# Local values in three key blocks of 96 rows by one load each, and the first expert loads a step later: a sparse attention with a mixture of experts on one core

## Chip, cores and metric

The kernel runs on one core of one Trainium2 chip. The metric is the device time of one execution in microseconds; before the change its median over three runs was 573.74 us (573.61 to 576.4).

## What is computed

Attention over 8 batches, 8 heads, 576 positions and head dimension 64, all in float32; then each token (4608 of 512 columns) goes to one of 8 experts, a two-layer network with a ReLU.

```python
mask_local = (rel >= 0) & (rel < 32)                      # heads 0 to 3
mask_strided = (rel >= 0) & (pos[None, :] % 32 == pos[:, None] % 32)   # heads 4 to 7
attn = softmax(where(mask, q @ k.T / 8, -1e9));  x = attn @ v
logits = x @ w_gate + modality_bias[modality_id];  e = argmax(logits)
out = softmax(logits)[e] * (relu(x @ w1[e]) @ w2[e])
```

A query of a local head sees 32 keys: those up to itself in its own block of 32, and the rest in the block before. A query of a strided head sees the 18 positions with its own remainder by 32.

## The kernel before

The program has two stages. In the first, attention is done in 32 units: for each of the four pairs of batches (`NBP`), four heads of `Local` and four units of `Strided`, in turns (even units are local, odd ones strided). TensorE's order is written out by hand: the loop `for n in range(nu + 3)` runs 35 steps, and step n holds the scores of unit n, the turning (transposes) of unit n - 2, the masks of unit n + 1 and the values of unit n - 3. Between these lie five places, 0 to 4; at places 0 to 3 `spot(n, place)` calls `fetch`, which issues the loads that the table `FETCH` names for that place, and `slot`. `pop` puts in pieces of `finish_pair` and `route`, which turn a finished pair of batches into token rows, compute the routing of its tokens and scatter them to `xd` in memory. The other engines are ordered by the scheduler, by its own estimate of times; the instructions inside `pin` keep the program's order.

In `FETCH`, "12a" and "12b" are the two halves (64 rows each) of unit 12's q and k, "12v" the first half of its values and "12w" the second half. Each load is issued on SyncE's queue (SP) and is `paced`: it waits for the last TensorE instruction ahead of it in the program. The values of a strided unit are one load of 128 rows; those of a local unit are two, over the odd and over the even rows.

A local unit's values (`vl`) are laid out in 18 windows of 65 columns (64 and a column of ones, which gives the sum of the weights). A window holds the 32 keys of the block before and the 32 of its own block. Windows of two neighbouring blocks lie above each other in 64 + 64 rows: block j - 1, block j, block j, block j + 1, so that block j is there twice. In `turn` of `Local`, the exponentials `ex` are transposed into PSUM (`t1` for 16 blocks, `t2` for the two left over), and ScalarE (ACT) copies them into `et` and `e8`, in which the first window's columns fill rows 0 to 63 and the second's rows 64 to 127; the rest of these tiles was set to zero once. `values` multiplies them by `vv`:

```python
et[r, :, :, par, :] <- t1[r]              # r = 64 rows, par = 0, 1
o[64 * jj:64 * jj + 64, k, :] = et[:, ...].T @ vv[:, 4 * k + 2 * jj + bb, :]
```

`SPOTS` says at which places a `slot` does something: it issues a piece of the scatter, or, once the first routing tables are known (`calm`), the next of ten pieces of `early`: the first experts' weights (`raws[0]` to `raws[3]`; the last two share their tiles with `lqk`) and the first tokens (`fx`). Steps 32 to 34, if not in the table, have places 1, 2 and 4.

The second stage runs the experts in blocks of 256 or 512 tokens (`ffn`), with each float32 operand split in a high and a low part: `h` (L1052) and `o` (L1070) are its matmuls, `wh` and `wl` (L1094, L1097) and, for the first block, `ws` (L975) the split weights.

Of the kernel before, what the change touches and what calls it, by code (L numbers as in the profile page):

```python
# [20 lines left out]
P = 128  # L21
B, H, S, D = 8, 8, 576, 64
STRIDE = 32
NBP = 4
# [15 lines left out]
LT, RK = 3, (13, 6)  # L40
SPOTS = {
    15: (2, 3, 4,), 16: (0, 1,), 18: (1,), 19: (2, 3, 4,), 23: (2, 3,), 25: (1, 2, 3,), 27: (2, 3, 4,), 28: (0,),
    29: (1, 2, 4,), 30: (0, 1,), 31: (1, 2, 4,),
}
FETCH = {
# [9 lines left out]
}  # L55
LAG = 2
FIRST, SECOND, SPLIT, SEND, GATHER, FAR = 1, 3, 4, 6, 7, 6
CPAD = 1216
BIG = -float(2 ** 30)
# [77 lines left out]
def _layout(q, k, v, moe_modality_id, moe_w_gate, moe_modality_bias, moe_w1, moe_w2):  # L137
    q, k, v = (np.asarray(t, np.float32) for t in (q, k, v))

    def local_t(t):
        return t[:, :4].reshape(NBP, 2, 4, S, D).transpose(0, 2, 1, 4, 3).reshape(NBP, 4, 2, D, 18, 32)

    qt, kt = local_t(q), local_t(k)
    vr = v[:, :4].reshape(NBP, 2, 4, 18, 32, D).transpose(0, 2, 1, 3, 4, 5)
    qkl = np.zeros((NBP, 4, 2, D, 37, 32), np.float32)
    win = np.zeros((NBP, 4, 2, 64, 18, D + 1), np.float32)
    win[..., D] = 1
    for bb in range(2):  # L150
        for i in range(18):
            blk = _block(i, bb)
            qkl[:, :, bb, :, i] = qt[:, :, bb, :, blk]
            qkl[:, :, bb, :, 19 + i] = kt[:, :, bb, :, blk]
            w = win[:, :, i % 2, :, 2 * (i // 2) + bb]
            w[:, :, 32:, :D] = vr[:, :, bb, blk]
            if blk:
                qkl[:, :, bb, :, 18 + i] = kt[:, :, bb, :, blk - 1]
                w[:, :, :32, :D] = vr[:, :, bb, blk - 1]
    qkl = np.stack([qkl[:, :, 1], np.concatenate([qkl[:, :, 0, :, 18:], qkl[:, :, 0, :, :18]], axis=-2)], axis=2)  # L160
    qkl = qkl.reshape(NBP, 4, P, 37 * 32)
    vl = win.reshape(NBP, 4, P, 18 * (D + 1))

    def strided_t(t):
        t = t[:, 4:].reshape(B, 2, 2, 18, 32, D).transpose(0, 1, 2, 5, 4, 3)
        return np.ascontiguousarray(t).reshape(B, 2, 2, D, S)

    qs, ks = strided_t(q), strided_t(k)
    qks = np.stack([np.concatenate([qs[:, :, 1], ks[:, :, 1]], axis=-1), np.concatenate([ks[:, :, 0], qs[:, :, 0]], axis=-1)],
                   axis=2).reshape(B, 2, P, 2 * S)  # L170

    vr = v[:, 4:].reshape(B, 2, 2, 18, 32, D)
    vs = np.zeros((B, 2, P, 10, D), np.float32)
    va = vr[:, :, :, :, 0:28].reshape(B, 2, 2, 18, 4, 7, D).transpose(0, 1, 5, 3, 4, 2, 6)
    vs[:, :, 0:126, 0:8] = va.reshape(B, 2, 126, 8, D)
    vb = vr[:, :, :, :, 28:32].transpose(0, 1, 4, 3, 2, 5)
    for u in range(4):
        vs[:, :, 32 * u:32 * u + 18, 8:10] = vb[:, :, u]
    vs = vs.reshape(B, 2, P, 10 * D)

    w1 = np.asarray(moe_w1).reshape(E, 4, P, 8, P).transpose(0, 3, 2, 1, 4).reshape(E, 8, P, 512)
    w2 = np.asarray(moe_w2).reshape(E, 8, P, DM)
    w = np.concatenate([w1, w2], axis=-1).reshape(E, 4, 2, P, 1024).transpose(0, 1, 3, 2, 4).reshape(E * 4 * P, 2048)

    wg = np.zeros((P, 4, 32), np.float32)
    wg[:, :, :E] = np.asarray(moe_w_gate).reshape(4, P, E).transpose(1, 0, 2)
    mod = np.ascontiguousarray(moe_modality_id).astype(np.int64).view(np.int32).reshape(NT, 2)[:, 0]
    mod = mod.reshape(36, P).transpose(1, 0)
    mb = np.broadcast_to(np.asarray(moe_modality_bias).reshape(1, 2 * E), (P, 2 * E))
    cf, cb, cr, tok = _constants()  # L190
    cz = np.concatenate([wg.reshape(P, 4 * 32), mb.astype(np.float32), np.ascontiguousarray(mod).view(np.float32),
                         tok.view(np.float32), np.ascontiguousarray(cr).view(np.float32)], axis=1)
    assert cz.shape == (P, Z_N)
    nul = np.zeros((SLOT, ROW), np.int32)
    nul[:, DM] = NT
    arrays = {
        "qkl": qkl, "vl": vl, "qks": qks, "vs": vs, "w": w,
        "cz": cz, "cf": cf, "cb": cb, "nul": nul.view(np.float32),
    }
    return {n: np.ascontiguousarray(t) for n, t in arrays.items()}  # L200
# [14 lines left out]
def attention_moe(ctx: ExitStack, tc: tile.TileContext, a, out):  # L215
# [140 lines left out]
    class Local:  # L356
# [7 lines left out]
            self.qk = lqk[n % 2]  # L364
            return load_qk(self.qk.rearrange("p x i q -> p (x i q)"), S + 32, a["qkl"][self.bp, self.h], part)

        def load_values(self, part):
            n = self.n
            if not part:
                self.vv = lp.tile([P, 18, D + 1], F32, tag="vv", name=f"vv{n}")  # L370
            return pin(nc.sync.dma_start(
                self.vv.rearrange("p i d -> p (i d)")[part:P:2], a["vl"][self.bp, self.h, part:P:2]))

        def masks(self):
            self.sp = []
# [40 lines left out]
        def turn(self):  # L416
            n, ex = self.n, self.ex
            self.et = et = ets[n % 2]
            t1 = pa(f"t1{n}").rearrange("p (g q) -> p g q", g=4)
            for k in range(4):  # L420
                turned_to(t1[:, k, :], ex[:, 2 * k:2 * k + 2, :])
            t2 = pa(f"t2{n}")[:, 0:P]
            turned_to(t2, ex[:, 8:10, :])
            for par in range(2):
                r = slice(64 * par, 64 * par + 64)
                nc.scalar.copy(et[r, :, :, par, :], t1[r].rearrange("p k (u q) -> p k u q", u=4))
            self.e8 = e8 = e8s[n % 2]
            for jj in range(2):
                r = slice(64 * jj, 64 * jj + 64)
                nc.scalar.copy(e8[r, :, jj, :], t2[r, r].rearrange("p (b q) -> p b q", b=2))  # L430

        def values(self):
            n, et, e8, vv, xt, h = self.n, self.et, self.e8, self.vv, self.xt, self.h
            for bb in range(2):
                gn = 5 - bb
                o = pa(f"o{n}{bb}")[:, :(D + 1) * gn].rearrange("p (g c) -> p g c", g=gn)
                for k in range(4):
                    for jj in range(2):
                        nc.tensor.matmul(  # L439
                            o[64 * jj:64 * jj + 64, k, :],  # L440
                            et[:, 2 * (k // 2) + bb, 2 * (k % 2) + jj, :, :].rearrange("p g q -> p (g q)"),
                            vv[:, 4 * k + 2 * jj + bb, :],
                            start=True, stop=True, skip_group_check=True,
                        )
                if bb == 0:
                    for b2 in range(2):
                        nc.tensor.matmul(
                            o[64 * b2:64 * b2 + 64, 4, :], e8[:, b2, :, :].rearrange("p j q -> p (j q)"),
                            vv[:, 16 + b2, :], start=True, stop=True, skip_group_check=True,
                        )  # L450
                rs = lp.tile([P, 5], F32, tag="rs", name=f"rs{n}{bb}")
                nc.vector.tensor_scalar(rs[:, :gn], o[:, :, D], 1e-9, None, ALU.add)
                nc.vector.reciprocal(rs[:, :gn], rs[:, :gn])
                nc.vector.tensor_tensor(
                    xt[bb][:, :, D * h:D * h + D], o[:, :, 0:D],
                    rs[:, :gn].unsqueeze(2).to_broadcast([P, gn, D]), ALU.mult,
                )

    class Strided:
# [7 lines left out]
            self.qk = sqk[n % 2]  # L467
            return load_qk(self.qk.rearrange("p i q -> p (i q)"), S, a["qks"][self.b, self.pr], part)

        def load_values(self, part):  # L470
            n = self.n
            self.vs = lp.tile([P, 10, D], F32, tag="vs", name=f"vs{n}")
            return pin(nc.sync.dma_start(self.vs.rearrange("p g d -> p (g d)"), a["vs"][self.b, self.pr]))
# [756 lines left out]
    def fetch(n, place):  # L1230

        for item in FETCH.get((n, place), "").split():
            u, part = units[int(item[:-1])], "abvw".index(item[-1])
            paced(u.load(part) if part < 2 else u.load_values(part - 2))

    for i in range(3):
        for part in range(2):
# [116 lines left out]
```

## Time and profile before

| | |
|---|---|
| runs | 573.61, 573.74, 576.4 us |
| the profiled execution | 577.81 us, its span 575.7 us |
| TensorE (PE), matmuls | 546.1 us busy, 95% |
| VectorE (DVE) | 378.6 us, 66% |
| ScalarE (ACT) | 312.2 us, 54% |
| GpSimd (POOL) | 89.0 us, 15% |
| data moved by DMA | 137.00 MB, 238 GB/s |
| mean granted clock of TensorE | 0.987 |

An engine's busy share is a mean over stages with different limits, so stages are looked at one by one. A wait is named by the engine, the line, and what ended it; "issue" is time in which the engine waited for nothing that the profile shows. PEld is TensorE's weight load, which runs beside its matmuls. The names behind a line are the tile written, an arrow, and the tiles read.

### The profile page before, as it was taken

How to read it: one execution, taken by the hardware profiler on the slowest of the kernel's cores; microseconds unless marked ns; L12 is line 12 of the kernel's file. 1: busy time of each engine (PE TensorE's matmuls, PEld its weight loads, DVE VectorE, ACT ScalarE, POOL GpSimd, SP SyncE). 2: the span in 40 equal slices, each digit the busy share in tenths (PEclk: the TensorE clock that was granted, in tenths of full speed). 3: DMA queues.
4: the chain of work that ended last, by engine and by line, in shares of the span. 5: the costliest groups of instructions: out<-in, count | busy, mean ns of one | idle time of the engine just before them, and what ended most of it. 6: DMA issues, size and time to landing. Idle time of an engine off the chain costs nothing.

```text
span 575.7 us, 13499 instructions
## 1 busy us (share of the span) xinstructions
PE 546.1 (95%) x5273; PEld 463.0 (80%) x5273; DVE 378.6 (66%) x940; ACT 312.2 (54%) x651; POOL 89.0 (15%) x108
## 2 busy tenths in 40 slices
PE   6888798898999999999999999999999999999995
PEld 3677687776888999899888888888888888889984
DVE  7886877868977996777875626735734634547541
ACT  3476586676776666666643344343353353356642
POOL 2020212320603511011010020020020020021320
PEclk9899999998999999999999999999999999999998
DMA  8888988989999999998996672582482543455621
GB/s 290 271 287 295 309 279 285 303 313 370 389 322 282 317 367 347 356 304 233 309 248 245 141 266 78 147 275 91 128 253 95 153 178 111 128 202 174 246 92 40
DMA packets 65942, 137.00 MB, mean 238 GB/s; under 512 B 40383, under 2 KB 40767, under 8 KB 58816
## 3 DMA queue, kind: packets, MB, share of 16 engines
q1 hardware_dynamic: 59168, 112.46, 61.1%
q0 software_dynamic: 6416, 23.37, 11.0%
q8 instruction: 43, 0.70, 0.5%
q10 hardware_dynamic: 288, 0.24, 0.1%
q14 instruction: 27, 0.22, 0.1%
HBM read 107.97 MB, written 24.30 MB: 230 GB/s over the span
## 4 chain that ended last, share of the span: by engine, by line
PE 86%; issue 4%; DVE 4%; ACT 3%; DMA 1%; POOL 0%; SPq 0%; POOLq 0%; DVEq 0%; ACTq 0%
PE h L1052 35%; PE o L1070 35%; PE o L439 2%; PE oa L535 2%; PE s L391 2%; PE lg L612 1%; PE xl L236 1%; PE t L236 1%; PE xs L236 1%; PE ss L485 1%; ACT xc L548 1%; DMA lqk<-in_qkl 1%; PE ts L236 1%; PE s L379 1%; DVE mx L404 0%
## 5 line engine op out<-in xcount | busy, mean ns | idle before, releaser
L1052 PE MATMUL h<-xh,wh 128*128 128x256 f32 (+1 forms) x408 | 133.0, 326 | 0.1
L1052 PE MATMUL h<-xh,wl 128*128 128x256 f32 (+1 forms) x408 | 132.8, 326 | 0.0
L1052 PE MATMUL h<-xl,wh 128*128 128x256 f32 (+1 forms) x408 | 132.6, 326 | 0.0
L1070 PE MATMUL o<-wh,h 128*128 128x512 f32 x320 | 105.8, 392 | 0.0
L1097 DVE TENSOR_TENSOR wl<-lqk,wh 128x512 fp32r<-128x512 f32 x104 | 67.9, 687 | 54.2 <-ACT wh L1094 52.0
L1094 ACT CAST wh<-raw 128x512 fp32r<-128x512 f32 x102 | 58.6, 621 | 61.6 <-PE o L1070 57.8
L1078 POOL DMA_INDIRECT out<-y,le x36 | 39.0, 1083 | 326.8 <-ACT y L1077 320.2
L1097 DVE TENSOR_TENSOR wl<-raw,wh 128x512 fp32r<-128x512 f32 x102 | 66.4, 687 | 35.0 <-ACT wh L1094 34.9
L1094 ACT CAST wh<-lqk 128x512 fp32r<-128x512 f32 x104 | 59.9, 619 | 49.2 <-PE o L1070 49.2
L1052 PEld LDWEIGHTS h<-xh,wh 128*128 128x128 f32 x408 | 77.3, 189 | 9.6 <-ACT wh L1094 0.3
L1052 PEld LDWEIGHTS h<-xl,wh 128*128 128x128 f32 x408 | 77.3, 189 | 9.1
L1052 PEld LDWEIGHTS h<-xh,wl 128*128 128x128 f32 x408 | 77.3, 189 | 7.7 <-issue 0.4
L1070 PEld LDWEIGHTS o<-wh,h 128*128 128x128 f32 x320 | 60.1, 188 | 13.6
L1070 PE MATMUL o<-wl,h 128*128 128x512 f32 x160 | 62.9, 393 | 0.0
L1061 DVE SCALAR_TENSOR_TENSOR h<-h,h 128x512 fp32r<-128x512 f32 x40 | 27.7, 691 | 47.3 <-ACT h L1060 47.3
L1060 ACT ACTIVATE h<-h 128x512 fp32r<-128x512 f32 x40 | 23.9, 598 | 50.2 <-PE h L1052 50.1
L1070 PE MATMUL o<-wh,hh 128*128 128x512 f32 x128 | 51.1, 399 | 0.0
L1070 PE MATMUL o<-wl,hh 128*128 128x512 f32 x128 | 50.5, 395 | 0.0
L1070 PE MATMUL o<-wh,hl 128*128 128x512 f32 x128 | 49.1, 393 | 0.0
L1060 ACT ACTIVATE hh<-h 128x256 fp32r<-128x256 f32 x64 | 24.6, 385 | 20.2 <-PE h L1052 19.8
L1070 PEld LDWEIGHTS o<-wl,h 128*128 128x128 f32 x160 | 30.0, 188 | 6.7
L1061 DVE SCALAR_TENSOR_TENSOR hl<-h,hh 128x256 fp32r<-128x256 f32 x64 | 26.7, 417 | 5.5 <-ACT hh L1060 5.4
(211 smaller groups left out, 841.7 us busy)
## 6 DMA issues: line engine op xcount, KB each, us to landing
lqk<-in_w SPq DMA_DIRECT2D x26, 1024.0 KB, 9.7
raw<-in_w SPq DMA_DIRECT2D x24, 1024.0 KB, 5.2
lqk<-in_qkl SPq DMA_DIRECT2D x32, 296.0 KB, 4.8
vv<-in_vl SPq DMA_DIRECT2D x32, 292.5 KB, 6.3
sqk<-in_qks SPq DMA_DIRECT2D x32, 288.0 KB, 6.0
fx<-xd SPq DMA_DIRECT2D x16, 528.0 KB, 3.9
vs<-in_vs SPq DMA_DIRECT2D x16, 320.0 KB, 5.3
xd<-in_nul SPq DMA_DIRECT2D x9, 528.0 KB, 9.4
```

Source lines behind the costliest of these rows:

```text
L236: nc.tensor.transpose(dst, src, ident)
L379: nc.tensor.matmul(sp, identb, cb[:, M_L + 64 * half:M_L + 64 * half + 64 * gn], start=True, stop=True)
L391: nc.tensor.matmul(sp[32 * u:32 * u + 32, 128 * m:128 * m + 128], q[:, i, :], kd[:, :, i:i + 2, :], start=False, stop=True, skip_group_che ...
L439: nc.tensor.matmul(o[64 * jj:64 * jj + 64, k, :], et[:, 2 * (k // 2) + bb, 2 * (k % 2) + jj, :, :].rearrange("p g q -> p (g q)"), vv[:, 4 ...
L535: nc.tensor.matmul(oa[64 * h:64 * h + 64, 126 * u:126 * u + 126], vs[0:126, 2 * u + h, :], eb[0:126, 4 * h + u, :, :].rearrange("p t q -> ...
L1052: nc.tensor.matmul(hp, wx[:, a1], x[:, c, :], start=(k == 0), stop=(k == 11))
L1060: evicted[f] = nc.scalar.activation(hh[:], hp, AF.Relu)
L1061: nc.vector.scalar_tensor_tensor(hl[:], hp, 0.0, hh.bitcast(F32), ALU.max, ALU.subtract)
L1070: nc.tensor.matmul(os[h], hx[:, m], w[:, 512:1024], start=(f == 0 and i == 0), stop=(f == 7 and i == 2))
L1078: outs.add(nc.gpsimd.indirect_dma_start(out, IOA(ap=le[:, 0:1], axis=0), y[:], None, bounds_check=NT - 1, oob_is_err=False))
L1094: ins = nc.scalar.copy(wh[:, c], raw[:, c])
L1097: nc.vector.tensor_tensor(wl[:, c], raw[:, c], wh[:, c].bitcast(F32), ALU.subtract)
```

## The change

The three key blocks of two neighbouring windows are now stored once each: `vl` has 96 rows (`KV`) instead of 128, block j - 1, block j and block j + 1, and is loaded by one DMA. The matmuls of `values` contract over 96 rows. The second window's weights have to stand in rows 32 to 95 instead of 64 to 127. Their copy from PSUM rows 64 to 127 is therefore split in two of 32 rows, in `et` and in `e8`. The items "w" are gone from `FETCH`, the others stand where they stood. In `SPOTS`, the slots from step 29 on are moved one to two steps back.

```diff
-    29: (1, 2, 4,), 30: (0, 1,), 31: (1, 2, 4,),
+    30: (1, 2,), 31: (0, 1, 2, 4,), 32: (1, 2, 4,), 33: (1,),
 FETCH = {
-    (0, 0): "3a 3b 0v", (1, 1): "0w 4a 4b", (1, 3): "1v 5a", (3, 2): "5b 2v 2w 6a 6b 3v",
+    (0, 0): "3a 3b 0v", (1, 1): "4a 4b", (1, 3): "1v 5a", (3, 2): "5b 2v 6a 6b 3v",
...
-    (25, 1): "24w 28a 28b 25v 29a 29b", (26, 2): "26v 26w 30a 30b", (27, 2): "27v 31a 31b", (28, 0): "28v",
-    (29, 0): "29v 28w", (30, 0): "30v 30w", (31, 0): "31v",
+    (25, 1): "28a 28b 25v 29a 29b", (26, 2): "26v 30a 30b", (27, 2): "27v 31a 31b", (28, 0): "28v",
+    (29, 0): "29v", (30, 0): "30v", (31, 0): "31v",
 }
+KV = 96
...
-    win = np.zeros((NBP, 4, 2, 64, 18, D + 1), np.float32)
+    win = np.zeros((NBP, 4, 3, 32, 18, D + 1), np.float32)
...
-            w = win[:, :, i % 2, :, 2 * (i // 2) + bb]
-            w[:, :, 32:, :D] = vr[:, :, bb, blk]
+            w = win[:, :, :, :, 2 * (i // 2) + bb]
+            w[:, :, 1 + i % 2, :, :D] = vr[:, :, bb, blk]
             if blk:
                 qkl[:, :, bb, :, 18 + i] = kt[:, :, bb, :, blk - 1]
-                w[:, :, :32, :D] = vr[:, :, bb, blk - 1]
+                if i % 2 == 0:
+                    w[:, :, 0, :, :D] = vr[:, :, bb, blk - 1]
...
-        def load_values(self, part):
+        def load_values(self):
             n = self.n
-            if not part:
-                self.vv = lp.tile([P, 18, D + 1], F32, tag="vv", name=f"vv{n}")
-            return pin(nc.sync.dma_start(
-                self.vv.rearrange("p i d -> p (i d)")[part:P:2], a["vl"][self.bp, self.h, part:P:2]))
+            self.vv = lp.tile([P, 18, D + 1], F32, tag="vv", name=f"vv{n}")
+            return pin(nc.sync.dma_start(self.vv.rearrange("p i d -> p (i d)")[0:KV], a["vl"][self.bp, self.h]))
...
-            for par in range(2):
-                r = slice(64 * par, 64 * par + 64)
-                nc.scalar.copy(et[r, :, :, par, :], t1[r].rearrange("p k (u q) -> p k u q", u=4))
+            for par, k0, kn in ((0, 0, 64), (1, 64, 32), (1, 96, 32)):
+                r, to = slice(k0, k0 + kn), slice(k0 - 32 * par, k0 - 32 * par + kn)
+                nc.scalar.copy(et[to, :, :, par, :], t1[r].rearrange("p k (u q) -> p k u q", u=4))
...
-                            et[:, 2 * (k // 2) + bb, 2 * (k % 2) + jj, :, :].rearrange("p g q -> p (g q)"),
-                            vv[:, 4 * k + 2 * jj + bb, :],
+                            et[0:KV, 2 * (k // 2) + bb, 2 * (k % 2) + jj, :, :].rearrange("p g q -> p (g q)"),
+                            vv[0:KV, 4 * k + 2 * jj + bb, :],
```

`e8` and the two matmuls that read it are changed in the same way.

On SP, at the beginning of the expert loads (`vv` are values of local, `vs` of strided units; `raw_2759` and `raw_2848` are the first expert's first weights in the kernel before and in the changed one; `TENSOR_LOAD` reads a row number for the loads behind it). Before:

```order
L371 DMA vv_2613<-in_vl 64x1170
L891 TENSOR_LOAD eb_2172
L902 ISA
L902 DMA raw_2759<-in_w 128x1024
L902 ISA
L902 DMA raw_2759<-in_w 128x1024
L856 TENSOR_LOAD row_2167
L861 ISA
L861 DMA fx_00_2809<-xd 128x528
L371 DMA vv_2811<-in_vl 64x1170 x2
L861 ISA
L861 DMA fx_00_2809<-xd 128x528
```

Now:

```order
L372 DMA vv_2810<-in_vl 96x1170
L891 TENSOR_LOAD eb_2182
L902 ISA
L902 DMA raw_2848<-in_w 128x1024
L902 ISA
L902 DMA raw_2848<-in_w 128x1024
L473 DMA vs_2894<-in_vs 128x640
L856 TENSOR_LOAD row_2177
L861 ISA
L861 DMA fx_00_2896<-xd 128x528
L861 ISA
L861 DMA fx_00_2896<-xd 128x528
```

The last local unit's values have moved ahead of the expert loads, and the last strided unit's values ahead of the tokens `fx`.

On ACT, at the end of the third pair of batches (`et`, `e` and `xc` are the copies out of PSUM, `lo` the exponential of the routing). Before:

```order
L426 COPY et_88<-t_2680 64x16x32 x2
L430 COPY e_90<-t_2685 64x2x32 x2
L414 ACTIVATE ex_2616<-ex_2616 128x384
L548 COPY xc_142<-oa_2693 128x28x18
L549 COPY xc_142<-ob_2702 128x4x18
L656 ACTIVATE lo_2659<-lo_2659 128x72
L525 ACTIVATE eb_2769<-ts_2764,cf_sb 126x8x18 x3
L501 ACTIVATE exs_2744<-exs_2744 128x288
```

Now:

```order
L426 COPY et_88<-t_2692 64x16x32
L426 COPY et_88<-t_2692 32x16x32 x2
L430 COPY e_90<-t_2697 64x2x32
L414 ACTIVATE ex_2628<-ex_2628 128x384
L430 COPY e_90<-t_2697 32x2x32 x2
L548 COPY xc_142<-oa_2707 128x28x18
L549 COPY xc_142<-ob_2716 128x4x18
L656 ACTIVATE lo_2671<-lo_2671 128x72
L525 ACTIVATE eb_2771<-ts_2766,cf_sb 126x8x18 x3
L501 ACTIVATE exs_2757<-exs_2757 128x288
```

Two copies are added ahead of `lo`, and one of the exponentials `ex` has moved ahead of the last copies of `e`.

On DVE at the same place (`sml` sums what ACT's `lo` gives, `eb` and `exs` belong to the strided units). Before:

```order
L495 TENSOR_REDUCE mxs_2742<-ss_2691 128x16
L658 TENSOR_REDUCE sml_2675<-lo_2659 128x9
L666 TENSOR_TENSOR cnt<-cum_2672,cnt 128x8
L521 TENSOR_TENSOR eb_2769<-ts_2764,cf_sb 126x8x72
L498 TENSOR_TENSOR exs_2744<-ss_2691,mxs_2742 128x8x2x18
L659 TENSOR_SCALAR sml_2675<-sml_2675 128x9
```

Now:

```order
L495 TENSOR_REDUCE mxs_2755<-ss_2705 128x16
L666 TENSOR_TENSOR cnt<-cum_2684,cnt 128x8
L521 TENSOR_TENSOR eb_2771<-ts_2766,cf_sb 126x8x72
L498 TENSOR_TENSOR exs_2757<-ss_2705,mxs_2755 128x8x2x18
L658 TENSOR_REDUCE sml_2687<-lo_2671 128x9
```

`sml`, which waits for ACT, has moved behind `eb` and `exs`. The same stands at the ends of the first two pairs. TensorE's order in the attention stage is the same as before.

## Rows read from the trace of the kernel before

**Rows 1.** The page: the span.

```profile
span 575.7 us, 13499 instructions
```

**Rows 2.** Stretches: length, busy us (instructions) of each engine, PE's clock, DMA share, GB/s.

```profile
0.00:145.70 145.70, 122.93 (x2985) 101.12 (x2985) 113.17 (x406) 93.25 (x236) 27.10 (x52) 0.96 0.88 301
145.70:575.70 430.00, 423.15 (x2292) 361.83 (x2288) 265.45 (x535) 218.96 (x416) 61.89 (x57) 0.99 0.68 217
```

**Rows 3.** What PE waited for, 0 to 146 us: total us, times, longest.

```profile
PE ss L485 <- issue: 3.7, 3, 2.1
PE s L391 <- issue: 3.6, 4, 1.7
PE o L439 <- issue: 3.5, 2, 1.9
PE ts L236 <- DVE ec L526: 2.4, 1, 2.4
PE lg L612 <- issue: 2.0, 2, 1.2
...
PE ts L236 <- DVE posi L677: 1.4, 2, 1.1
PE lg L617 <- issue: 0.9, 1, 0.9
PE oa L535 <- issue: 0.8, 1, 0.8
PE s L391 <- DMA lqk<-in_qkl: 0.8, 2, 0.4
```

**Rows 4.** Stretches from stall to next stall: length, PE busy (matmuls), clock, DMA share, GB/s.

```profile
26.75:32.82 6.07, 4.48 (x126) 1.00 0.95 322
32.82:37.30 4.48, 4.24 (x126) 1.00 0.81 245
37.30:44.57 7.27, 6.44 (x125) 1.00 0.90 292
...
60.73:68.22 7.49, 4.49 (x125) 1.00 0.94 324
130.78:137.04 6.26, 3.82 (x127) 1.00 0.96 316
sum 37.60, PE 28.59; mean PE 4.76
```

**Rows 5.** DMA from 0 to 150 us: issues, KB each, median us to landing.

```profile
DMA packets 13497, 45.92 MB, mean 306 GB/s; under 512 B 2314, under 2 KB 2698, under 8 KB 13202
...
q8 instruction: 23, 0.38, 1.1%
...
vv<-in_vl SPq DMA_DIRECT2D x32, 292.5 KB, 6.3
...
vs<-in_vs SPq DMA_DIRECT2D x16, 320.0 KB, 5.3
...
lqk<-in_w SPq DMA_DIRECT2D x2, 1024.0 KB, 11.3
```

**Rows 6.** Matmuls by form, 0 to 146 us: busy us, mean ns, idle before.

```profile
L439 PE MATMUL o<-vv,et 128*64 128x65 f32 x512 | 22.6, 234 | 3.5 <-issue 3.5
```

**Rows 7.** ACT by form, 0 to 146 us.

```profile
L426 ACT COPY et<-t 64x512 f32<-64x512 f32 x32 | 18.5, 578 | 12.9 <-PE t L236 12.5
...
L525 ACT ACTIVATE eb<-ts,cf_sb 126x144 f32<-126x144 f32 x48 | 14.9, 391 | 8.9 <-DVE eb L521 8.8
...
L414 ACT ACTIVATE ex<-ex 128x256 f32<-128x256 f32 x16 | 6.7, 420 | 16.8 <-DVE ex L409 16.7
L430 ACT COPY e<-t 64x64 f32<-64x64 f32 x32 | 6.6, 206 | 0.7
```

**Rows 8.** ACT's timeline: start us, us, instruction, idle before.

```profile
140.41 1.18 ACT L426 COPY et<-t 64x512 f32<-64x512 f32 x2 [0.78 <-PE t L236]
...
144.72 0.62 ACT L975 CAST ws<-raw 128x512 fp32r<-128x512 f32 x1
```

**Rows 9.** What DVE waited for, 0 to 145 us.

```profile
DVE sms L503 <- ACT exs L501: 2.6, 4, 0.9
DVE sml L658 <- ACT lo L656: 2.2, 3, 0.7
```

**Rows 10.** SP's timeline at the first expert load.

```profile
130.06 0.96 SPq L902 DMA_DIRECT2D raw<-in_w  x2
```

More of the change, by code (lines that the diff above doesn't have):

```diff
@@ L154, in _layout @@
             qkl[:, :, bb, :, 19 + i] = kt[:, :, bb, :, blk]
-            w = win[:, :, i % 2, :, 2 * (i // 2) + bb]
-            w[:, :, 32:, :D] = vr[:, :, bb, blk]
+            w = win[:, :, :, :, 2 * (i // 2) + bb]
+            w[:, :, 1 + i % 2, :, :D] = vr[:, :, bb, blk]
             if blk:
                 qkl[:, :, bb, :, 18 + i] = kt[:, :, bb, :, blk - 1]
-                w[:, :, :32, :D] = vr[:, :, bb, blk - 1]
+                if i % 2 == 0:
+                    w[:, :, 0, :, :D] = vr[:, :, bb, blk - 1]
     qkl = np.stack([qkl[:, :, 1], np.concatenate([qkl[:, :, 0, :, 18:], qkl[:, :, 0, :, :18]], axis=-2)], axis=2)
     qkl = qkl.reshape(NBP, 4, P, 37 * 32)
-    vl = win.reshape(NBP, 4, P, 18 * (D + 1))
+    vl = win.reshape(NBP, 4, KV, 18 * (D + 1))
     def strided_t(t):
@@ L423, in turn @@
             turned_to(t2, ex[:, 8:10, :])
-            for par in range(2):
-                r = slice(64 * par, 64 * par + 64)
-                nc.scalar.copy(et[r, :, :, par, :], t1[r].rearrange("p k (u q) -> p k u q", u=4))
+            for par, k0, kn in ((0, 0, 64), (1, 64, 32), (1, 96, 32)):
+                r, to = slice(k0, k0 + kn), slice(k0 - 32 * par, k0 - 32 * par + kn)
+                nc.scalar.copy(et[to, :, :, par, :], t1[r].rearrange("p k (u q) -> p k u q", u=4))
             self.e8 = e8 = e8s[n % 2]
-            for jj in range(2):
-                r = slice(64 * jj, 64 * jj + 64)
-                nc.scalar.copy(e8[r, :, jj, :], t2[r, r].rearrange("p (b q) -> p b q", b=2))
+            for jj, k0, kn in ((0, 0, 64), (1, 64, 32), (1, 96, 32)):
+                r, to = slice(k0, k0 + kn), slice(k0 - 32 * jj, k0 - 32 * jj + kn)
+                nc.scalar.copy(e8[to, :, jj, :], t2[r, 64 * jj:64 * jj + 64].rearrange("p (b q) -> p b q", b=2))
         def values(self):
@@ L447, in values @@
                         nc.tensor.matmul(
-                            o[64 * b2:64 * b2 + 64, 4, :], e8[:, b2, :, :].rearrange("p j q -> p (j q)"),
-                            vv[:, 16 + b2, :], start=True, stop=True, skip_group_check=True,
+                            o[64 * b2:64 * b2 + 64, 4, :], e8[0:KV, b2, :, :].rearrange("p j q -> p (j q)"),
+                            vv[0:KV, 16 + b2, :], start=True, stop=True, skip_group_check=True,
                         )
@@ L468, in load, with load_values @@
             return load_qk(self.qk.rearrange("p i q -> p (i q)"), S, a["qks"][self.b, self.pr], part)
-        def load_values(self, part):
+        def load_values(self):
             n = self.n
@@ L1232, in fetch @@
         for item in FETCH.get((n, place), "").split():
-            u, part = units[int(item[:-1])], "abvw".index(item[-1])
-            paced(u.load(part) if part < 2 else u.load_values(part - 2))
+            u, part = units[int(item[:-1])], "abv".index(item[-1])
+            paced(u.load(part) if part < 2 else u.load_values())
     for i in range(3):
```

12 rows, old and new, of the table FETCH are left out of this document.

## Prediction

> **What bounds the kernel now.** I read first the span cut in two at 145.7 us, where the first expert matmul starts. In the attention stage PE is busy 122.93 of 145.70 us, in the expert stage 423.15 of 430.00 us [rows 1, 2]. Behind 145.7 us PE has next to nothing to give back, and the change takes no instruction from it there; whatever it does is decided in the 22.8 us that PE idles before.
>
> Next I read what PE waits for in that stage [rows 3]. The reader is to see three things. Missing data is hardly there: 0.8 us, on the first loads of q and k, and no row for the values. VectorE is there with 2.4 us once and 1.4 us in two. The largest part, 13 waits with 3.7 + 3.6 + 3.5 + 2.0 + 0.9 + 0.8 = 14.5 us, is "issue": PE stops, and nothing that the profile shows releases it.
>
> Third, the stage cut at the ends of such stalls [rows 4]. From one stall to the next PE runs 126 matmuls (127 in the last piece), whether that takes 4.48 or 7.49 us; with a weight load for each that is 252 instructions and a few that are not counted. So I take these waits for PE's own program arriving in blocks, a little late. The profile counts a queue for instructions among the DMA queues, 23 packets and 0.38 MB in these 150 us [rows 5], so the blocks come through the same DMA engines as the data, and these engines are at a busy share of 0.81 to 0.97 in the six pieces. From one stall to the next neighbouring one takes 37.60 / 6 = 6.27 us; a block that is late by a stall has taken about that long, and 6.3 us is also the median time of a values load from issue to landing [rows 5]. The DMA queue therefore reaches PE by its program, not by its data.
>
> [...]
>
> **The change, part by part.**
>
> *Fewer bytes.* 32 loads of 292.5 KB become 16 of 96/128 x 585 = 438.75 KB: 9,360 KB against 7,020, so 2.34 MB less of the 45.92 MB moved in 150 us, 5.1% [rows 5]. The least this can be worth is nothing, since PE waits for no value; the most, if the stage goes at the pace of the DMA engines, is 2.34 MB at 306 GB/s = 7.6 us. Between these I take the rows nearest to it, those of the blocks: 5.1% of 6.27 us is 0.32 us a block, times 13 stalls = 4.2 us. It can only help a block while a values load is in flight, 16 x 6.3 = 101 of 145.7 us, 0.69. So **-2.9 us**.
>
> *Fewer DMA issues.* 16 fewer on SP. SP's queue waits for PE at almost every load (each is paced behind a PE instruction), so this is hidden: 0.
>
> *Matmuls over 96 rows.* The count, the columns and the weight loads stay; only the contraction has 96 rows. No row here prices that. The ends are nothing and a quarter of the 22.6 us of the L439 group [rows 6], -5.6 us. I take 0, as the only row for this form is that of the unchanged column count; the end stays for the range.
>
> *More copies on ACT.* For each of the 16 local units one more copy of 512 columns (578 ns) and one of 64 (206 ns): 16 x 0.784 = 12.5 us of ACT work [rows 7]. What hides it is ACT's own waiting: it idles 16.7 us for `ex` from VectorE, 12.5 us for the turned tiles from PE and 8.8 us for `eb` [rows 7]. In three places that cover is thin. (a) The last local unit's copies start at 140.41 us and ACT then runs almost without a gap to the split of the first expert weights at 144.72 [rows 8], which the first expert matmul needs: **+0.8 us**. (b) At the end of the first three pairs VectorE waits for `lo` of ACT, 2.2 us in 3 times [rows 9]. `lo` now comes 0.78 us later, but the scheduler has put `sml` behind `eb` and `exs` on VectorE (above), which fills the wait: 0, between -2.2 and +2.3 (3 x 0.78). (c) VectorE waits for `exs` of ACT 2.6 us in 4 times [rows 9], and PE for VectorE three times, 2.4 and 1.4 us [rows 3]; the bound is 4 x 0.78 = 3.1 us, the other end nothing, as PE's next stall may swallow it. I take one such delay: **+0.8 us**.
>
> *Expert loads later.* The ten pieces of the first two blocks' weights and tokens go from step 29 to step 30 and on. A step lasts 145.7 / 35 = 4.2 us, so the first, now issued at 130.06 [rows 10], goes at about 134.3 at the latest. It lands 5.3 us (the 320 KB row, nearest to its 512 KB) to 11.3 us (the 1,024 KB row) later [rows 5]: 139.6 to 145.6, needed at 144.72 [rows 8]. Cost 0 to 0.9; I take 0. In return the queue is emptier where PE has its longest wait, 2.4 us in front of `ts` of the last steps [rows 3]; that piece is one of those that end at a block [rows 4]. Between 0 and -2.4 I take a quarter, **-0.6 us**, since a values load and a token load move into the gap.
>
> Sum: -2.9 + 0.8 + 0.8 - 0.6 = **-1.9 us**. The profiled execution took 577.81 us (span 575.7, 2.1 around it), 4.1 above the median of 573.74, so it would go to 575.9; the median to **571.8 us**. A measurement of this kernel tells about 0.5% from no change, 2.9 us, so my forecast is a small gain inside that.
>
> **The rivals.**
>
> *DMA sets the pace (566.9 us).* If the blocks and the loads share one saturated queue, the whole 7.6 us come back, less the 0.8 of (a): 573.74 - 6.8. For it: a share of 0.88 or so over the stage [rows 2], and stalls that lie in the fuller pieces. Against it: only 0.8 us of waiting for loads [rows 3]; a saturated queue would show there first.
>
> *The load is no shorter (574.7 us).* Landing does not follow the bytes here: 292.5 KB take 6.3 us, 320 KB over 128 rows 5.3 us [rows 5]. If a load of 96 rows holds its fullest lane as long as two of 64 did, the relief is nil, and +0.8 + 0.8 - 0.6 = +1.0 us stay. The same comes out if a block is late for its own length, not for the queue. For it: the 4.48 us piece has the lower share, 0.81, but 7.27 us came at 0.90 and 6.07 at 0.95 [rows 4], so share alone doesn't order them. [...] No row here shows a load of 96 rows.
>
> *ACT comes onto the path (slower, 577.1 to 580.0 us).* The mechanism: the turned tiles stay in their PSUM buffers and `exs` comes later by 0.78 us, VectorE's `ens` with it, and PE stands at `ts`. It decides where the ACT queue has no idle left in a step: the three pair ends, the four `exs` waits and the last unit, 8 x 0.78 = 6.3 us; with the relief 573.74 + 6.3 - 2.9 = 577.1, without it 580.0. For it: ACT goes from 93.25 [rows 2] to 105.8 us of 145.7. Against it: over 37 us of waiting on others [rows 7].
>
> **How the numbers follow.** Forecast 0.43, DMA pace 0.20, load no shorter 0.22, ACT 0.15. Faster by over 0.5% (below 570.9): the DMA case and a third of the forecast, where the relief is 4.2 and the last wait goes whole: 0.20 + 0.14 = 0.34. Slower (above 576.6): the ACT case and a little of the second: 0.18. Within: 0.48. The range reaches from 566.5 (the DMA case; the matmul end gives about the same, 571.8 - 5.6) to 577.5 (the ACT case with relief); outside lie the parts beyond, some 0.08 on either side.
>
> **What would show it.** Right: values loads x16 of 438.75 KB; "issue" waits of PE before 145 us falling from 14.5 to about 11 us, still every 126 matmuls; ACT busy in the attention stage up by 12 us; `sml` waiting less than 0.7; the first expert matmul at about 144. Wrong: "issue" unchanged or larger (the second rival); `ts` of PE waiting for `ens` or ACT in several steps (the third); the copies of 32 rows costing other than 578 and 206 ns; a wait of `ws` or `wh` for expert weights behind 143 us.

## The result, and the profile after

The changed kernel takes 583.0 us (median of 4, 581.66 to 583.53), the kernel before 574.65 in the same runs (median of 4, 573.61 to 576.4): slower, ratio 1.0118 with a 95% interval of 1.0074 to 1.0162. The profiled execution took 583.53 us. That of before [rows 1] was 3 us above its median, so the two spans lie closer together, 5.7 us, than the medians. Executions over 1.5% longer than the fastest of their kernel are left out of the ratios and the half-clock times below.

The span of the page, and two stretches, cut where the first expert matmul starts (length, busy us of PE, PEld, DVE, ACT, POOL, PE's granted clock, DMA share, GB/s):

```profile
span 581.4 us, 13503 instructions
```

```profile
0.00:148.40 148.40, 126.38 (x2986) 102.14 (x2986) 112.48 (x406) 104.39 (x268) 24.94 (x50) 0.95 0.85 272
148.40:581.40 433.00, 423.54 (x2291) 361.88 (x2288) 264.92 (x535) 218.63 (x416) 66.78 (x59) 1.00 0.69 218
```

A profile is one execution. A second one of the kernel before, used below, reached its first expert matmul at 140.84 us, 4.9 earlier than in [rows 2]:

```profile
0.00:140.84 140.84, 120.08 (x2985) 97.66 (x2986) 113.66 (x407) 93.69 (x238) 28.48 (x53) 1.00 0.89 306
```

So what two profiles differ by is taken as an effect of the change only where other runs have it too.

Against [rows 2]: 2.7 us of the 5.7 are lost before the first expert matmul and 3.0 behind it. Setting the two traces side by side matmul by matmul (PE has 5273 in both), the distance is 2.7 us at the 3,000th and the 3,120th, 5.7 us at the 3,240th, and 5.7 us at the last. So the kernels run alike only after some 185 us, 40 us later than the prediction had it, and most of the 3.0 us are these waits:

```profile
PE rk L671 <- DVE ohb L652: 1.7, 1, 1.7
PE h L1052 <- DVE wl L1097: 0.9, 1, 0.9
```

`rk` ranks the tokens of the last pair. ACT is busy 104.39 us in the first stretch, 11.1 more than before, about as forecast (12). What PE waits for there:

```profile
PE ss L485 <- DMA sqk<-in_qks: 4.1, 3, 1.6
PE ss L485 <- issue: 3.8, 3, 2.6
PE s L391 <- issue: 3.1, 3, 2.3
...
PE lg L612 <- ACT xc L549: 1.5, 3, 0.6
...
PE lg L612 <- issue: 0.9, 1, 0.9
PE s L391 <- DMA lqk<-in_qkl: 0.8, 2, 0.4
PE lg L612 <- ACT xc L570: 0.7, 2, 0.3
PE o L439 <- DMA vv<-in_vl: 0.6, 1, 0.6
PE o L439 <- issue: 0.4, 1, 0.4
...
PE lg L617 <- issue: 0.3, 1, 0.3
```

"Issue" is 8.5 us here and 14.5 in [rows 3], a larger fall than forecast. But it was 11.1 in the second profile of the kernel before, and 8.5 in a run below that has the new places of the expert loads alone, so the fall is not shown to come from the fewer bytes. PE idles 148.40 - 126.38 = 22.0 us, where it idled 22.8 and, in the second profile, 20.8. There are 5.5 us of waits for loads of `sqk`, `lqk` and `vv` (1.1 and 2.8 in the two profiles of before); two close relatives of the changed kernel, the runs called rows and scatter below, have only 1.7 and 1.6. The 2.2 us of `lg` for ACT's `xc` (none in either profile of before) come back, with 1.5 to 2.2 us, in all runs with the split copies on ACT.

What is longer in the stage is PE's busy time: 126.38 us, and 126.1 and 125.0 in rows and scatter, against 122.93 and 120.08, for the same matmuls. The granted clock of 0.95 is a part of that: in the changed kernel 13.2 us of the busy time are at half clock, in the two profiles of before 10.0 and 0. Five `t` matmuls of the changed kernel take 0.77 us at full clock (from 26.43 us) and 1.33 at half (from 36.30); so if half of these times is counted as lost, an estimate, the clock explains about half of the 3.5 us to the first of them and all of the 6.3 to the second.

The values' loads, from 0 to 150 us, and the main load queue from 0 to 140 us (packets, MB, time of its packets as a share of 16 engines):

```profile
vv<-in_vl SPq DMA_DIRECT2D x16, 438.8 KB, 6.4
vs<-in_vs SPq DMA_DIRECT2D x16, 320.0 KB, 6.4
```

```profile
q1 hardware_dynamic: 9383, 32.04, 73.3%
```

For before the same view has

```profile
q1 hardware_dynamic: 10729, 35.99, 76.4%
```

The strided values, which nobody changed, land in 6.4 us where they took 5.3 [rows 5], though in rows and scatter in 5.6 and 5.4. And the queue's packets now take 0.733 x 140 x 16 / 32.04 = 51.2 us of one engine per MB, against 47.5; by the same sum it is 47.1 in the second profile of before, 50.5 and 51.9 in rows and scatter. A byte has become dearer.

Matmuls and copies by form, 0 to 146 us (busy us, mean ns, idle before):

```profile
L439 PE MATMUL o<-vv,et 96*64 96x65 f32 x512 | 21.9, 232 | 1.0 <-DMA vv<-in_vl 0.6 <-issue 0.4
...
L426 ACT COPY et<-t 32x512 f32<-32x512 f32 x32 | 18.5, 578 | 0.8
L426 ACT COPY et<-t 64x512 f32<-64x512 f32 x16 | 9.2, 574 | 11.1 <-PE t L238 10.9
...
L430 ACT COPY e<-t 32x64 f32<-32x64 f32 x32 | 6.5, 204 | 0.7
```

A matmul over 96 rows takes 232 ns, over 128 it took 234 [rows 6]; half the rows cost a copy all of its time, 578 and 204 ns [rows 7].

### The profile page after: what moved, and what is told of

It reads as the page before. It is cut to its first block, busy times and chain, and to the rows that moved or that the text cites. A ratio compares the mean times of both kernels' runs of the same rounds, so it can differ in the third digit from the quotient of the medians.

```text
span 581.4 us, 13503 instructions
## 1 busy us (share of the span) xinstructions
PE 549.9 (95%) x5273; PEld 464.0 (80%) x5273; DVE 377.4 (65%) x940; ACT 323.0 (56%) x683; POOL 91.7 (16%) x108
## 4 chain that ended last, share of the span: by engine, by line
PE 78%; DMA 6%; DVE 6%; issue 4%; ACT 3%; POOL 0%; SPq 0%; POOLq 0%; DVEq 0%; ACTq 0%
PE h L1052 32%; PE o L1070 32%; PE o L439 2%; DMA xd<-xb,posi 2%; PE s L391 2%; DMA fx<-xd 2%; PE oa L535 1%; DMA vv<-in_vl 1%; DMA sqk<-in_qks 1%; PE ss L485 1%; DVE wl L1097 1%; PE t L238 1%; PE xs L238 1%; PE xl L238 1%; ACT xc L548 1%
## 5 line engine op out<-in xcount | busy, mean ns | idle before, releaser
L1060 ACT ACTIVATE hh<-h 128x256 fp32r<-128x256 f32 x64 | 24.6, 384 | 21.2 <-PE h L1052 20.8
L426 ACT COPY et<-t 32x512 f32<-32x512 f32 (+1 forms) x48 | 27.7, 577 | 11.9 <-PE t L238 10.9
```

What stands on the lines that cost most here:

```text
L426: nc.scalar.copy(et[to, :, :, par, :], t1[r].rearrange("p k (u q) -> p k u q", u=4))
L1060: evicted[f] = nc.scalar.activation(hh[:], hp, AF.Relu)
```

## The experiments

The kernel before ran beside the experiments, in five groups. It took 574.6, 589.6, 590.8, 576.4 and 574.4 us there, so kernels of different groups are compared by their ratio to it. "Half clock" is the time lost to it: one minus the mean granted clock, times the span, averaged over the executions of the kernel.

**The parts of the change.** Is it the places of the expert loads, or the 96 rows, and in these the copies?

```diff
 # spots: the kernel before, new SPOTS alone
+    30: (1, 2,), 31: (0, 1, 2, 4,), 32: (1, 2, 4,), 33: (1,),
 # rows: the changed kernel with the SPOTS of before
-    30: (1, 2,), 31: (0, 1, 2, 4,), 32: (1, 2, 4,), 33: (1,),
+    29: (1, 2, 4,), 30: (0, 1,), 31: (1, 2, 4,),
 # scatter: the changed kernel, third pair's scatters at places 1, 2 and 4 of steps 33 and 34
+        if n > nu and place in (1, 2, 4):
+            scatter_rows(1)
 # copies: the kernel before, the second copies of et and e8 split
-            for par in range(2):
+            for par, k0, kn in ((0, 0, 64), (1, 64, 32), (1, 96, 32)):
```

> The kernel before with the new SPOTS alone (values still by two loads of 64 rows). Theory A: the slots of the expert loads push the nine scatters of the third pair behind them; the last goes at about 161 us instead of 154, the first tokens of the second phase come 12 us later, and PE stands 2 to 3 us around 180 us: 577 to 580 us. Theory B (the added ACT copies cost the time) and theory C (the 96-row load does): as the kernel before, 573.5 to 576 us, last scatter near 154 us.

> The changed kernel with the old SPOTS: only the 96 rows, the one load and the split copies. Theory A: the stall around 180 us is gone and the last scatter is back at 154 to 157 us; what is left is what the attention stage lost, 2 to 4 us: 576 to 579 us. Theories B and C: nearly all stays, 581 to 584 us.

> The changed kernel, expert loads where it has them, but the third pair's scatters at places 1, 2 and 4 of steps 33 and 34 as before. Theory A: 3 us come back, 579 to 580.5 us, no wait of VectorE for fx near 175 us. Theories B and C: as the changed kernel, 582 to 584 us. If the delay of the expert loads itself costs (theory D), also 582 to 584 us, with a wait of ws, wh or the first rows for a DMA.

> The kernel before with each second copy of et and e8 split in two of 32 rows, all else as before: 12.5 us more of ACT. Theory A: hidden nearly whole, 574 to 576 us. Theory B: 578 to 583 us, with PE waiting for ACT or for ens in several steps. Theory C: as before.

Measured: new places alone 0.9984 [0.9942, 1.0026]; the 96-row part alone 1.0122 [1.0072, 1.0173]; the changed kernel with the third pair's scatters put forward again 1.0115 [1.007, 1.0159]; split copies alone 1.0044 [1.0002, 1.0085]. The loss is in the 96-row part as far as the intervals tell, and the scatters have no share that shows. The 1.7 us wait of `rk` stands in the profile of the new places too, and the median does not feel it.

Where the copies cost is seen at the end of the first pair, on ACT, in the changed kernel (start us, us, instruction):

```profile
46.68 1.77 ACT L426 COPY et<-t 64x512 f32<-64x512 f32 x3
48.47 0.65 ACT L430 COPY e<-t 64x64 f32<-64x64 f32 x3
49.15 0.52 ACT L414 ACTIVATE ex<-ex 128x384 f32<-128x384 f32 x1
49.70 1.01 ACT L548 COPY xc<-oa 128x504 f32<-128x504 f32 x1
50.51 0.32 ACT L549 COPY xc<-ob 128x72 f32<-128x72 f32 x1
```

and on PE at the same time:

```profile
50.88 1.07 PE L612 MATMUL lg<-xc,cz_sb 128*32 128x256 f32 x16 [0.61 <-ACT xc L549]
52.28 0.41 PE L612 MATMUL lg<-xc,cz_sb 128*32 128x256 f32 x2 [0.33 <-ACT xc L570]
```

Three `et` copies and three `e` copies stand in ACT's queue ahead of `xc`, and PE's routing matmuls `lg` stop until `xc` is there. The run with the split copies alone has the same waits in the same three places:

```profile
PE lg L612 <- ACT xc L549: 1.3, 3, 0.6
PE lg L612 <- ACT xc L570: 0.9, 3, 0.3
```

The copies reach VectorE as well, by `exs`. In the changed kernel, 0 to 148 us, against 2.6 us in 4 times in [rows 9]:

```profile
DVE sms L503 <- ACT exs L501: 9.8, 9, 2.0
```

With the split copies alone it is 9.4 us; in runs without them, the second profile of before (4.5) and the new places (5.2) among them, it is at most 5.2. Little of it gets to PE: its wait for `ens` is 2.2 us both in the changed kernel and with the split copies alone, and 1.5 and 2.3 in the two profiles of before.

**The load, and where it lies.** What is left of the 96-row part?

```diff
 # load96: the 96-row part, copies not split, SPOTS of before
 # onedma128: the kernel before, values by one DMA, items "w" gone
-                self.vv.rearrange("p i d -> p (i d)")[part:P:2], a["vl"][self.bp, self.h, part:P:2]))
+            return pin(nc.sync.dma_start(self.vv.rearrange("p i d -> p (i d)"), a["vl"][self.bp, self.h]))
 # two96: rows part:96:2, two DMAs at the places of before, split copies, SPOTS of before
 # padded: the 96-row part, SPOTS of before, vl with 128 rows in memory
+            ... self.vv.rearrange("p i d -> p (i d)")[0:KV], a["vl"][self.bp, self.h, 0:KV]))
```

> The 96-row layout by one DMA, but the two copies behind the turns as they were (two of 64 rows, each in its own place) and the loads of the expert weights where they were before. The products over 96 rows of the odd blocks then see the wrong rows, so half of the local values are left wrong; the work per instruction is that of the changed kernel but for the copies. Known so far: all of the 96-row part costs +8 us, the split copies alone +2.5 us. Theory L (the load itself, one transfer of 96 rows instead of two of 64, costs the other 5.5): 579 to 581 us. Theory K (the load costs nothing; the copies cost 8 when they stand in a program with fewer of the other stalls): 573 to 575.5 us. Theory M (the inputs behind the local values lie elsewhere in memory): 579 to 581 us, like L.

> The kernel before, with its 128-row layout and all of its bytes, but each unit's values by one DMA of 128 rows, at the place of the first half; the second halves' places are left out. 16 fewer issues, no other row of the order moved. Theory L1 (it is the one transfer in place of two that costs, by what it queues ahead of the next unit's queries and keys, or by what it does to the order of the loads): 578 to 581 us. Theory L2 (it is the 96 rows) and theory M (memory): 573.5 to 575.5 us, as before. Theory K: as before or 1 us faster.

> The 96-row layout with the split copies, but by two DMAs of 48 rows at the places of before; the loads of the expert weights where they were before. Theory L1 (one transfer in place of two): 576 to 578 us, the copies' share alone. Theory L2 (96 rows, however they are moved), theory M and theory K: 580 to 583 us, like the 96-row part with one DMA (582.6).

> The 96-row part as in the run with the old places (582.6 us, same order of instructions row by row), but the array of local values keeps 128 rows in device memory, of which 96 are read, so that every later input keeps the address that it had before. Theory M (the weights and inputs behind it land later because of where they lie): 576 to 578 us, and the landing of the query and key loads after 160 us back from 10 to 5 us. Theories L1, L2 and K: 581 to 584 us.

Measured, against 589.57 us: the load of 96 rows without split copies 1.0109 [1.0047, 1.017]; one transfer of 128 rows, all bytes kept, 1.0107 [1.0049, 1.0166]; 96 rows by two transfers, with split copies, 1.007 [1.003, 1.0109]; padded 1.0109 [1.0031, 1.0186]. Load96 leaves the second window's weights in rows 64 to 127, so the products of the odd blocks are not the right ones; its work per instruction is that of the 96-row part without the added copies. Padded leaves the memory places no share that shows. One transfer in place of two costs 1% by itself, although on PE, DVE, ACT and POOL the order of every instruction is that of before, and 96 rows in it cost what 128 do: the bytes saved bring nothing that shows. With 96 rows by two transfers less of the cost is left, 0.7% with the copies, which cost 0.44% alone; but its interval overlaps those of the other three. Load96 and padded differ by the split copies and come out alike, so within the 96-row kernel the copies' price does not show. One transfer of 128 rows loses 13.3 us to half clock, the kernel before 7.9 (14.3 and 8.8 over all executions); the rest of their time, 580.4 and 579.9 us, is nearly the same.

**Smaller transfers, and the copies on another engine.**

```diff
 # four32: four DMAs, rows k:128:4
+                self.vv.rearrange("p i d -> p (i d)")[k:P:4], a["vl"][self.bp, self.h, k:P:4]))
+                for k in (part, part + 2)]
 # vs_halves: the strided values in two halves of every second row
+                self.vs.rearrange("p g d -> p (g d)")[k:P:2], a["vs"][self.b, self.pr, k:P:2])) for k in range(2)]
 # copies_dve, two96_dve: split copies (128 rows, and two96), those of rows 96 to 127 on VectorE
+                (nc.vector.tensor_copy if k0 == 96 else nc.scalar.copy)(...
```

> The kernel before, all of its bytes, but each unit's local values by four DMAs of 32 rows (every fourth row), two at each of the two places of before; 32 issues more. One DMA of 128 rows cost 6 us, all of it as half clock (14.3 us lost against 8.8). Theory P (the size of the piece: the sequencer's program packet waits behind the piece in flight, and a long stall pulls the clock down): less time at half clock than before, 570 to 573 us by the scale of a before of 574.6, ratio 0.990 to 0.998. Theory Q (it is the count of issues that are under way, the fewer the worse, by the eight completion semaphores that loads take in turn): as P or better in the attention stage. Theory S (one issue costs the SP queue about 0.6 us, and loads are late when there are more of them): ratio 1.003 to 1.015, with waits of PE for lqk, sqk and vv landings.

> The kernel before with the strided units' values (one DMA of 128 rows, 320 KB) as two DMAs of 64 rows at the same place; 16 issues more, the local values as they were. Theory P: a little faster than before, ratio 0.993 to 0.999, with less time at half clock. Theory S: ratio 1.001 to 1.006. If only pieces over 500 KB matter: 1.000.

> The kernel before with the second copies behind the turns split in two of 32 rows, as in the run that did this on ScalarE (ratio 1.0044), but the new third copies (rows 96 to 127) on VectorE. Theory A1 (ScalarE's time: the copies delay the next exponents and the xc copies that PE waits for): ratio 0.998 to 1.002. Theory A2 (what follows the turn has one more thing to wait for, wherever it is done): 1.003 to 1.007. VectorE is busier than ScalarE in this stage (113 against 93 of 146 us), so a price there of the same size would come out as A2.

> The 96-row layout by two DMAs of 48 rows at the places of before, the third copies on VectorE; the expert weights' loads as before. With theory A1 and the load's share gone by using two DMAs: ratio 0.994 to 1.001, the fewer bytes now bringing up to 3 us. With A2: 1.003 to 1.007, as with the copies on ScalarE (1.0070).

Measured, against 590.83 us: four transfers 0.9996 [0.9965, 1.0026]; strided halves 0.9967 [0.9928, 1.0006], no difference that shows; third copies on VectorE 1.0165 [1.0121, 1.0208], with 96 rows 1.0181 [1.0139, 1.0223]. Transfers smaller than 292 KB gain nothing that shows, and 32 issues more cost nothing. Both theories on the copies missed: on VectorE they cost nearly four times what they cost on ACT. There they stand ahead of `ens`, for which PE waits at `ts`. In the kernel before that row has 1.5 us; with the copies on VectorE, 0 to 150 us:

```profile
PE ts L236 <- DVE ens L507: 11.5, 4, 3.1
```

**Size, count, or which rows.** The large transfer still differed in several ways from the two.

```diff
 # 112_16, 64_64, 96_32: two DMAs of neighbouring rows (split at 112, 64 or 96)
+            r = slice(112, P) if part else slice(0, 112)
+                self.vv.rearrange("p i d -> p (i d)")[r], a["vl"][self.bp, self.h, r]))
 # one_vs_halves: onedma128 and vs_halves together
 # halves_spots: vs_halves and spots together
```

> The kernel before with each unit's local values by two DMAs at the places of before, but of 112 and 16 rows instead of 64 and 64: count of issues, bytes and order as before, one transfer of 512 KB. Theory P (size): ratio 1.006 to 1.012, with more time at half clock, as with one DMA of 128 rows (1.0107). Theory Q (count of issues): 0.998 to 1.003.

> The kernel before with the local values by one DMA of 128 rows (1.0107 alone) and the strided values by two of 64 rows (0.9967 alone), so that a pair of units has seven loads again. Theory P: 1.005 to 1.011. Theory Q: 0.996 to 1.002.

> The kernel before with the strided values by two DMAs of 64 rows (0.9967 alone) and the changed kernel's places of the first expert loads (0.9984 alone); 128 rows and the copies as before. If the two add up: 0.993 to 0.999. If the first was chance: 0.997 to 1.001.

> The kernel before, unchanged, for a profile on this chip. Ratio 1.000; by both theories fewer waits of 2 us and more in the attention stage, and less time at half clock, than in the runs with one large transfer.

> The kernel before with each unit's local values by two DMAs of 64 neighbouring rows (0 to 63, 64 to 127) instead of the even and the odd rows; count, bytes and places as before. Theory P (size of the transfer): ratio 0.997 to 1.003. Theory N (neighbouring rows are what costs): 1.007 to 1.012.

> The kernel before with each unit's local values by two DMAs of 96 and 32 neighbouring rows; the first is as large as the changed kernel's (438.75 KB). Theory P: 1.003 to 1.012, between the even halves (1.000) and 112 with 16 rows (1.0125). Theory N: as with 64 and 64 neighbouring rows.

All of these runs but the one with the new places have the order of before on PE, DVE, ACT and POOL, word for word. "Packet" is the duration of a 4,680-byte packet (one row of local values) from 0 to 140 us, worked out from the trace. The last three rows have the split copies too.

| local values by | ratio | half clock, that of before beside it (us) | packet, median / mean (ns) |
|---|---|---|---|
| the even and the odd rows (before) | 1 | | 181 / 226 |
| the same, run again | 1.0012 [0.9969, 1.0054] | 5.0, 5.1 | 181 / 218 |
| every fourth row, four | 0.9996 [0.9965, 1.0026] | 8.6, 9.1 | |
| one of 128 | 1.0107 [1.0049, 1.0166] | 13.3, 7.9 | 181 / 227 |
| one of 128, strided ones halved | 1.0122 [1.0073, 1.0171] | 10.3, 5.1 | 181 / 225 |
| rows 0 to 111, 112 to 127 | 1.0125 [1.0064, 1.0185] | 9.3, 5.1 | 256 / 275 |
| rows 0 to 95, 96 to 127 | 1.0143 [1.0087, 1.0199] | 10.8, 5.2 | 267 / 281 |
| rows 0 to 63, 64 to 127 | 1.0132 [1.0074, 1.0191] | 8.0, 5.2 | 311 / 305 |
| rows 0 to 95 alone (the changed kernel) | 1.0118 [1.0074, 1.0162] | | 198 / 265 |
| the same, places of before (rows) | 1.0122 [1.0072, 1.0173] | 7.4, 5.4 | 195 / 260 |
| even and odd rows of 0 to 95 (two96) | 1.007 [1.003, 1.0109] | 9.7, 7.9 | 181 / 258 |

The run with 64 and 64 neighbouring rows decides: count, size, bytes, places and order are those of before, only the rows of each transfer are others, and it costs 1.3%. So size, which had looked settled by the two runs before it, does not explain this. Nor are neighbouring rows of device memory what is slow: each load of the local q and k takes 64 neighbouring rows of memory into every second partition, and its packet, of 4,736 bytes, takes 182 ns in the kernel before. It is the partitions that are written. A packet takes 311 ns instead of 181, and the queue's packets, 0 to 140 us, take more time for fewer bytes than before (76.4% for 35.99 MB, above):

```profile
q1 hardware_dynamic: 9888, 33.48, 82.1%
```

Two effects are to be kept apart. A transfer that writes a neighbouring part of the partitions (64, 96 or 112 of them) has slower packets by the median; over every second of 96 the median stays at 181 ns, though the mean is 258. In the three split runs the median falls as the first part takes in more of the partitions: 311 ns with 64, 267 with 96, 256 with 112. Why it matters which partitions a transfer writes is not shown. And one transfer of 128 rows has packets as fast as before, in two runs, and loses over 1% all the same, nearly all of it as half clock (some 5.3 of 5.8 us and of 6.2). With neighbouring rows half clock is 2.8 to 5.6 of 6.4 to 8.5 us, and PE idles 25.7 to 29.1 us before the first expert matmul, against 22.8 and 20.8. The count of issues is ruled out by the run with halved strided values. Whether its size or the order of its rows is behind it was not separated. The changed kernel's transfer of 96 rows has the first effect, and may have the second.

Several of the slower loads show in the stalls. The longest "issue" wait of PE up to 146 us is 2.1 us in [rows 3] and 1.9 in the second profile of the kernel before:

```profile
PE s L391 <- issue: 3.9, 3, 1.9
```

It is 3.4 us with 112 and 16 rows and 3.2 with 96 and 32. With 64 and 64 rows, and with one transfer and strided halves, it is the last number of these:

```profile
PE s L392 <- issue: 11.0, 4, 4.9
```

```profile
PE s L389 <- issue: 6.1, 3, 3.7
```

The changed kernel and its two relatives are no clear case of it, with 2.6, 2.3 and 2.3 us: the split copies and the strided halves, which lose less or nothing, have 2.4 and 2.6.

The 3.7 us one on PE's timeline, with two stretches of that run (columns as above: the 0.50 and 1.00 are the granted clock):

```profile
131.48 0.41 PE L389 MATMUL s<-lqk 128*32 128x128 f32 x4
135.63 1.19 PE L389 MATMUL s<-lqk 128*32 128x128 f32 x26 [3.73 <-issue]
```

```profile
131.60:135.63 4.03, 0.29 (x5) 0.03 (x3) 2.38 (x12) 1.39 (x6) 0.00 (x0) 1.00 0.98 385
136.20:139.40 3.20, 3.20 (x39) 2.66 (x32) 2.61 (x9) 1.00 (x2) 0.00 (x0) 0.50 0.73 220
```

While PE stands, the DMA engines are busy to 0.98. From 131.6 to 133.4 us no packet of the instruction queue runs; one starts at 133.42, ends at 134.35, and PE goes on 1.28 us later. The view of the queues from 133.4 to 134.4 us:

```profile
q8 instruction: 1, 0.02, 5.8%
```

Then the clock is at half (0.50 from 136.2 to 139.4 us), and five `t` matmuls from 137.17 us on take 1.33 us of PE, against 0.77 from 142.60 us on. That PE waited for its program, as the prediction took it, is well borne out: its 31 waits of over 2 us between 10 and 146 us, in all profiles but the two with copies on VectorE, end 1.20 to 1.64 us after such a packet of 16,384 bytes. The clock is what the prediction left out. That the packet itself waited behind data is inferred from these times; no run isolates it, and none shows what it waited for.

**No version beats both.** The two parts that stood at or under 1 alone, strided halves and new places, gave 1.0109 [1.0055, 1.0164] together: a miss, and its cause is open. It matters for the rest: this run has packets as fast as before (181 / 215 ns) and no transfer larger than before, so a loss of 1% can come by a way that was not found. That it is the loads in the others rests on their number: ten kernels with one transfer or with neighbouring rows lost 1.07 to 1.43%. No version is clearly faster than the kernel before.

## Why the prediction was wrong

It forecast 571.8 us (566.5 to 577.5) and gave slower a chance of 0.18; the median is 583.0.

*What bounds the kernel.* Right in part: PE's idle time ahead of the expert matmuls has its largest part in "issue", and that is PE's program arriving, as far as the long waits tell (1.20 to 1.64 us after a program packet). But not all is decided in those 22.8 us: of the 5.7 us between the two profiles 3.0 fall behind the first expert matmul, and ahead of it PE's busy time grew by 3.5 us while its idle time fell by 0.8. The inference that relief of "issue" is relief of the stage was wrong: it was 6 us less, and the idle time stayed.

*Fewer DMA issues, "this is hidden: 0".* This is the step that failed. Two transfers over every second row became one over rows 0 to 95, and only the count of issues was priced; the other shape of the transfer was put at nothing without a reason. The one transfer alone costs 1.0107, some 6 us, and 96 rows in one as much (1.0109). Which rows a transfer writes is shown to matter (1.0132 for halves of neighbouring rows); why one transfer of all 128 costs as much is open.

*Fewer bytes, -2.9 us.* Mis-sized, in two ways. The 6.27 us "that a block has taken" is the distance between stalls: the program's own packets in that trace last 0.9 to 1.8 us each, mean 1.1, so 5.1% of one is under 0.1 us. And it took the time of a load to follow its bytes. The values' packets from 0 to 140 us took 2048 x 226 ns = 463 us of one engine before and 1536 x 265 = 407 now; over 16 engines that is 3.5 us. The packets of the local q and k, unchanged in number and size, went from 221 to 241 ns and took 2.6 us of it back. Nor did what was left reach the run: with one transfer, 128 rows cost 1.0107 and 96 rows 1.0109.

*Matmuls over 96 rows, 0.* Right: 232 against 234 ns.

*More copies on ACT, +1.6 us.* Measured +2.5 us (0.44% of 574.6; interval 0.1 to 4.9). The durations of 578 and 204 ns and the sum on ACT were right, the place was not: (b) looked at `sml`, which indeed waits less (0.9 us against 2.2 in [rows 9]), and passed over `xc`, which stands in the same piece of ACT's order and which PE itself waits for, 2.2 us in all. (c) bounded the delay by 3.1 us; VectorE's wait for `exs` went from 2.6 (4.5 in the second profile) to 9.8, and little of that reached PE.

*Expert loads later, -0.6 us.* Not contradicted, and not shown either: -0.9 us (-3.3 to +1.5). The text did not count that the same table moves the third pair's scatters; two runs find no price for that.

*The rivals.* "The load is no shorter" came nearest: 96 rows gained nothing over 128. Its price stopped at no gain, where the transfer costs 1%. That a load has a fullest lane is shown by no run; what the runs showed is that one transfer cost 1.0109 with 96 rows and 1.0107 with 128. ACT on the path was real, with 2.5 of the 6.3 us, though the interval reaches down to 0.1. The parts, 1.09% for the load and 0.44% for the copies, come to 1.53% against 1.22% for both; the intervals are too wide to tell whether they add.

## What to carry to other kernels

A load that is cut in parts is best cut so that each part is spread over the partitions: here every second or every fourth row cost nothing that shows (0.9967 for the strided values, 0.9996 for the local ones), the first and the second half 1.3% (1.0132). Merging loads is a change of its own and wants its own term: one transfer for two cost 1% (1.0107) with all bytes and the order kept. Leaving a quarter of the partitions empty saved no run time here, and no matmul time either (232 against 234 ns). A copy is priced by its engine's queue: look for what stands behind it there and whether TensorE waits for that; moved to the busier engine, VectorE, it cost more here (1.0165 against 1.0044).

## What the runs showed of the hardware

In its long stalls PE went on 1.20 to 1.64 us after a program packet had ended (134.35 to 135.63, 33.70 to 35.02 and 34.84 to 36.18 us, for example, in three runs). Slow packets came with slower ones elsewhere: with 64 and 64 rows the q and k packets, which were not touched, took 258 ns in the mean instead of 217 to 221. And the kernel before took 574 to 577 us in three of the groups and 590 in two; its mean granted clock, 0.990 against 0.985, is some 3 us of that. It has no profile of its own in those two, but five of the eight other kernels' profiles there have one wait of 4.2 to 6.0 us of the first expert matmuls for `wh`, the split weights, and in the other groups none is longer than 1.3 us. What delayed `wh` is open.
